# Filling the prologue of a fused attention and feed-forward kernel: eight gate matmuls and one block's transposes moved beside the last scores, another block transposed by DMA, loads two blocks ahead

## The chip, the cores and the metric

The kernel runs on one core of one Trainium2 chip. The metric is the device time in microseconds (us), the median of several executions. A profiled execution also has a span, from its first to its last instruction, about 2 us less than the time. Engines are named as in the profile: PE is TensorE (matmuls), PEld its weight loads, DVE VectorE, ACT ScalarE, POOL GpSimd, SP SyncE, which issues most of the transfers.

Each execution also has a mean granted clock of PE. Most have 0.998 to 1.000 ("full clock" below). Some have 0.991 to 0.996 and take about 1 to 2 us longer, for the same kernel. All are counted as fast, so ratios include them.

## The reference

Sigmoid attention (8 batches, 12 heads, 448 positions, 64 per head), then a gated feed-forward layer with 768 model columns and 1536 hidden ones:

```python
scores = q @ k.T / sqrt(64) - log(448)
attn   = sigmoid(scores)
x      = (attn @ v)  # heads side by side: 3584 tokens x 768
out    = (relu(x @ w_gate) * (x @ w_val)) @ w_out
```

Inputs and the result are float32; the kernel computes in float16 with float32 accumulation. What matters here: attention is one sigmoid for each score, so ACT is busy with it, while the feed-forward part is almost all PE work.

## The kernel before

The 12 heads of a batch are three blocks of four heads; block n belongs to batch n // 3. The scores of a block come in seven chunks; chunk c of block n is one "step". Before any feed-forward product of batch 0 can be finished, the 21 steps of blocks 0, 1 and 2 must be done: this is the prologue. Then the feed-forward part of batch b runs on PE, with the attention steps of batch b+1 placed between its matmuls.

A block must be loaded, cast to float16 and transposed (k and q) before its first score. Blocks 0 to 6 were transposed on PE, later ones by DMA.

```python
def feed(i):                      # after attention step i
    n, c = divmod(i, NCH)         # NCH = 7 steps to a block
    m = n + LOAD_AHEAD            # LOAD_AHEAD = 3
    if c == 0 and NPRO <= m < NB: # NPRO = 6
        load_all(m)
    m = n + 1
    if c == 0 and NPRO <= m < NB:
        cast_block(m)             # on POOL
    if c == 4 and NPRO < m < NB:
        dma_transposes(m)
    if c == 5 and NBLK < m <= NPRO:
        transposes(m, "k")        # 7 on PE into PSUM, one DVE copy out
        transposes(m, "q")

# ... cut: loads of blocks 0 to 2, casts of block 0
order = halves("g", 0) + halves("u", 0) + [3] + halves("g", 1) + ...   # g, u, o: w_gate, w_val, w_out; a number: a block

for i in range(NP0 + 2):          # the prologue, NP0 = 21
    n, c = divmod(i, NCH)
    if n < NBLK:
        scores(n, c)              # 4 matmuls, then a sigmoid on ACT
    while done <= i - (4 if i < NP0 - 4 else 2):
        values(done // NCH, [done % NCH])
        done += 1
    # ... cut: casts and transposes of blocks 1 and 2
    if 13 <= i < NP0:
        start_next()              # the next load of "order", and its cast

# feed-forward of batch b
for step, cost in enumerate(ffn(b)):
    t += cost
    if b == 0 and step == 12:     # block 3
        transposes(NBLK, "k")
        transposes(NBLK, "q")
    # ... cut: starts loads, and places attention steps by t
```

One PSUM pool of four banks (`wkp`) serves the transposes, the value accumulators (two a block), and the gate, value and output products. A tile of the pool gets a bank only when the last reader of its old tile is done, and PE takes its matmuls in program order: one that waits for a bank (in a run below for 0.33 us) holds up all that stand behind it.

Of the kernel before, what the change touches and what calls it, by code (L numbers as in the profile page):

```python
# [9 lines left out]
FP32 = mybir.dt.float32  # L10
FP16 = mybir.dt.float16
AOP = mybir.AluOpType
AF = mybir.ActivationFunctionType
# [3 lines left out]
def kernel(  # L17
# [10 lines left out]
    nc = tc.nc  # L28

    B, H, S, D = q.shape  # L30
    DM, DF = moe_w_gate.shape
    P = 128
    HB = 4
    NBLK = H // HB
# [58 lines left out]
    def load_all(n: int):  # L93
        load_block(n, ("k", k, 0, NCH, nc.sync), ("q", q, 0, NCH, nc.sync), ("v", v, 0, NCH, nc.sync))
# [45 lines left out]
    def dma_transposes(n: int):  # L140
        for nm in ("k", "q"):
            h16 = qk16.pop((nm, n))
            t2 = qkTp.tile([P, NCH, 2, KC], FP16, tag="qkT", name=f"{nm}T")
            nc.sync.dma_start_transpose(
                t2[:].rearrange("p c h k -> p c (h k)"), h16[:].rearrange("p c r d -> p (c r d)")
            )
            qkT[nm, n] = t2

    def transposes(n: int, nm: str, *engines, cut=(0, NCH)):
        h16 = qk16.pop((nm, n))  # L150
        tr = wkp.tile([P, NCH, 2, KC], FP16, tag="wk", name="tr")
        for c in range(cut[0], cut[-1]):
            nc.tensor.transpose(tr[:, c], h16[:, c, :, :], ident[:])  # L153
        t2 = qkT.get((nm, n)) or qkTp.tile([P, NCH, 2, KC], FP16, tag="qkT", name=f"{nm}T")
        for c0, c1, eng in zip(cut, cut[1:], engines or (nc.vector,)):
            if eng is nc.scalar:
                eng.copy(t2[:, c0:c1], tr[:, c0:c1])
            else:
                eng.tensor_copy(t2[:, c0:c1], tr[:, c0:c1])
        qkT[nm, n] = t2  # L160
# [22 lines left out]
    def values(n: int, chunks):  # L183
        if chunks[0] == 0:
            PT[n] = [wkp.tile([P, 512], FP32, tag="wk", name="pv_ps") for _ in range(2)]
        pv = PT[n]
        t = v16[n]
        for c in chunks:
            pt = PT.pop((n, c))
            for pr, r, o in ((0, 0, 0), (0, 64, 64), (1, 64, 0), (1, 0, 64)):  # L190
                nc.tensor.matmul(  # L191
                    pv[pr][o : o + 64, 0:S],
                    t[r : r + 64, pr, c * D : (c + 1) * D],
                    pt[r : r + 64, pr, :],
                    start=(c == 0),
                    stop=(c == NCH - 1),
                    tile_position=(r, o),
                    skip_group_check=True,
                )
        if chunks[-1] == NCH - 1:  # L200
            b, i = divmod(n, NBLK)
            for pr in range(2):
                x = xTp.tile([P, S], FP16, tag="xT", name="xT")
                nc.vector.tensor_scalar(  # L204
                    out=x[:], in0=pv[pr][:, 0:S], scalar1=XSCALE, scalar2=None, op0=AOP.mult
                )
                xT[b, 2 * i + pr] = x
            PT.pop(n)
            v16.pop(n)
# [1 line left out]

    MM_US = 0.189

    def up(b: int, f: int):
        j, jj = divmod(f, FG)
        ps = []
        for w in (wg[j], wv[j]):
            acc = wkp.tile([P, 512], FP32, tag="wk", name="gv_ps")
            for dc in range(NDC):
                nc.tensor.matmul(  # L220
                    acc[:, 0:S],
                    w[:, dc, jj * P : (jj + 1) * P],
                    xT[b, dc][:],
                    start=(dc == 0),
                    stop=(dc == NDC - 1),
                )
                if dc < NDC - 1:
                    yield MM_US
            ps.append(acc)
            if len(ps) == 1:  # L230
                g_sb = gsbp.tile([P, S], FP32, tag="gsb", name="gate_sb")
                nc.scalar.activation(g_sb[:], acc[:, 0:S], AF.Relu)  # L232
                yield MM_US
        o = (b % NHALF) * S
        nc.vector.tensor_tensor(  # L235
            out=hT[f][:, o : o + S], in0=g_sb[:], in1=ps[1][:, 0:S], op=AOP.mult
        )
        yield MM_US

    def down(col0: int):  # L240
# [37 lines left out]

    def ffn(b: int):
        for f in range(NFC):  # L280
            yield from up(b, f)
        for col0 in blocks128(b):
            yield from down(col0)

# [1 line left out]
        return NFC * 2 * NDC * MM_US + len(blocks128(b)) * NFC * (DM / 2400.0 + 0.004)  # L286


    LOAD_AHEAD = 3
    NPRO = 2 * NBLK  # L290

    def cast_block(n: int):
        cast_qk(n, "q", nc.gpsimd)
        cast_qk(n, "k", nc.gpsimd)
        cast_v(n, nc.gpsimd)

    def feed(i: int):

        n, c = divmod(i, NCH)
        m = n + LOAD_AHEAD  # L300
        if c == 0 and NPRO <= m < NB:
            load_all(m)
        m = n + 1
        if c == 0 and NPRO <= m < NB:
            cast_block(m)
        if c == 4 and NPRO < m < NB:
            dma_transposes(m)
        if c == 5 and NBLK < m <= NPRO:
            transposes(m, "k")
            transposes(m, "q")  # L310

    state = {"pass": NBLK * NCH}
    def visit():
# [26 lines left out]
    with tc.manual_schedule():  # L340
        nc.scalar.activation(warm[:], bias_t[:], AF.Sigmoid)

        sp, act = nc.sync, nc.scalar
        load_block(0, ("q", q, 0, NCH, sp), ("k", k, 0, 4, act), ("k2", k, 4, NCH, sp), ("v", v, 0, NCH, act))
        load_block(1, ("k", k, 0, NCH, sp), ("q", q, 0, NCH, act), ("v", v, 0, NCH, sp))
        load_block(2, ("k", k, 0, NCH, act), ("q", q, 0, NCH, sp), ("v", v, 0, NCH, sp))

        def halves(kind, j):
            return [(kind, j, 0), (kind, j, 1)]

        order = halves("g", 0) + halves("u", 0) + [3] + halves("g", 1) + halves("u", 1)
        order += [4] + halves("g", 2) + halves("u", 2) + halves("o", 0) + [5]
        order += halves("o", 1) + halves("o", 2)

        def start_next():
            what = order.pop(0)
            if isinstance(what, int):
                load_all(what)
                cast_block(what)
            else:  # L360
                load_w(*what)
                cast_w(*what, nc.gpsimd)

        new_fill()
        filler(*[512] * 10)
        cast_qk(0, "q", nc.vector, nc.scalar, cut=(0, 4, NCH))
        cast_qk(0, "k", nc.vector, nc.scalar, cut=(0, 2, 4))
        transposes(0, "q")
        filler(128, 128)
        transposes(0, "k", nc.scalar, nc.vector, cut=(0, 2, 4))  # L370
        new_fill()
        filler(128, 128, 128)
        cast_qk(0, "k2", nc.vector, cut=(4, NCH))
        for n in range(NBLK):
            cast_v(n, nc.gpsimd)
        for _ in range(4):
            start_next()


        NP0 = NBLK * NCH  # L380
        done = 0
        for i in range(NP0 + 2):
            n, c = divmod(i, NCH)
            if n < NBLK:
                scores(n, c)
# [3 lines that stand above are left out]
            if i == 2:  # L389
                qk16["k", 0] = qk16.pop(("k2", 0))  # L390
                transposes(0, "k", nc.vector, cut=(4, NCH))
            if 1 <= i <= 3:
                filler(256)
            if c == 1 and n + 1 < NBLK:
                cast_qk(n + 1, "k", nc.vector)
                cast_qk(n + 1, "q", nc.vector)
            if c in (3, 5) and n + 1 < NBLK:
                transposes(n + 1, "k" if c == 3 else "q")
            if 13 <= i < NP0:
                start_next()  # L400

        for b in range(B):
            total = ffn_us(b)
            todo = []
            if b + 1 < B:
                count = 3 * NBLK + (2 if b == 0 else 0)
                lo = 4.0 if b == 0 else 0.0
                todo = [lo + (k + 0.5) * (total - lo) / count for k in range(count)]
            t = 0.0
            for step, cost in enumerate(ffn(b)):  # L410
                t += cost
                if b == 0 and step == 12:
                    transposes(NBLK, "k")
                    transposes(NBLK, "q")
                if order and step % 8 == 0:
                    start_next()
                if todo and t >= todo[0]:
                    todo.pop(0)
                    visit()
            for _ in todo:  # L420
                visit()
# [29 lines left out]
```

## Time and profile before

| | before |
|---|---|
| time, median of 3 | 434.99 us (434.75 to 435.08) |
| span of the profiled execution | 432.7 us, clock 0.999 |
| PE busy | 421.4 us, 97% |
| prologue: start of the last values | 26.75 us |
| first output matmul | 62.60 us |
| last cast of w_out | 65.96 to 67.43 us |

The prediction shows most lines of the profile. The page's second part, from which it starts, divides the span into 40 slices and gives the busy share of each engine in tenths.

### The profile page before, as it was taken

What the parts mean: (1) busy time and instruction counts of PE and PEld (TensorE: products, weight loads), DVE (VectorE), ACT (ScalarE), POOL (GpSimd) and SP (SyncE); (2) the same over time, 40 slices, a digit from 0 to 9 for tenths busy, and PEclk for the clock granted to TensorE, in tenths of its full rate; (3) what the DMA queues carried; (4) which work ended last, traced back from release to release, by engine and by line L of the source; (5) the groups of instructions that cost most, each with busy time, mean ns of one, the idle gap of its engine ahead of it and who ended that gap; (6) DMA issues with size and microseconds to landing.
All of it is one profiled execution on the core that took longest, in us unless ns stands there. A gap on an engine that the chain in (4) does not pass through costs nothing.

```text
span 432.7 us, 7894 instructions
## 1 busy us (share of the span) xinstructions
PE 421.4 (97%) x3296; PEld 214.6 (50%) x3296; DVE 99.5 (23%) x168; ACT 235.4 (54%) x325; POOL 105.6 (24%) x139
## 2 busy tenths in 40 slices
PE   7789999999999999999999999999999999999996
PEld 3344455544555445544455445554455544455554
DVE  3432332132202222122211233023220232212210
ACT  5955656655556656555546555565555556532221
POOL 2687669222301403113021133013030100000000
PEclk9999999999999999999999999999999999999999
DMA  8999997891238920695217932299114320030014
GB/s 302 385 385 385 388 394 261 229 268 46 42 77 238 300 45 2 172 244 163 42 42 198 251 126 44 53 234 294 22 21 111 79 44 2 17 94 1 2 36 111
DMA packets 62516, 66.52 MB, mean 154 GB/s; under 512 B 33936, under 2 KB 52752, under 8 KB 62480
## 3 DMA queue, kind: packets, MB, share of 16 engines
q1 hardware_dynamic: 61232, 64.17, 50.8%
q10 hardware_dynamic: 1248, 1.84, 1.2%
q8 instruction: 26, 0.43, 0.4%
q14 instruction: 10, 0.08, 0.1%
HBM read 47.19 MB, written 11.01 MB: 134 GB/s over the span
## 4 chain that ended last, share of the span: by engine, by line
PE 86%; DMA 6%; ACT 3%; POOL 2%; issue 1%; DVE 1%; SPq 0%; DVEq 0%; POOLq 0%
PE gv_ps L220 47%; PE y_ps L252 25%; PE qk_ps L167 8%; PE pv_ps L191 6%; DMA st_wo<-in_moe_w_out_dram 5%; ACT PT L177 3%; DMA st_k<-in_k_dram 2%; POOL wo L137 1%; PE tr L153 0%; POOL wg L137 0%; DVE xT L204 0%; SPq L90 0%; DVE h16q L105 0%; POOL v L112 0%; POOL v L114 0%
## 5 line engine op out<-in xcount | busy, mean ns | idle before, releaser
L177 ACT ACTIVATE PT<-qk_ps,bias_t 128x896 f16<-128x896 f32 x168 | 158.1, 1011 | 58.5 <-PE qk_ps L167 58.5
L220 PE MATMUL gv_ps<-xT,wv 128*128 128x448 f16 x576 | 127.8, 353 | 0.0
L220 PE MATMUL gv_ps<-xT,wg 128*128 128x448 f16 x576 | 127.4, 353 | 0.2 <-DVE xT L204 0.2
L252 PE MATMUL y_ps<-wo,hT 128*128 128x512 f16 (+2 forms) x684 | 114.5, 323 | 0.4 <-POOL wo L137 0.4
L232 ACT ACTIVATE gate_sb<-gv_ps 128x448 f32<-128x448 f32 x96 | 52.3, 544 | 91.6 <-PE gv_ps L220 91.6
L235 DVE TENSOR_TENSOR hT<-gate_sb,gv_ps 128x448 f16<-128x448 f32 x96 | 59.6, 621 | 168.1 <-PE gv_ps L220 137.5
L252 PEld LDWEIGHTS <-hT 128*128 128x128 f16 x684 | 64.2, 98 | 48.6 <-issue 8.2
L220 PEld LDWEIGHTS <-wv 128*128 128x128 f16 x576 | 54.6, 98 | 57.3 <-issue 8.6
L220 PEld LDWEIGHTS <-wg 128*128 128x128 f16 x576 | 54.9, 98 | 53.5 <-issue 5.7
L112 POOL CAST v<-st_v 128x448 f16<-128x448 f32 x24 | 13.5, 562 | 180.4 <-PE pv_ps L191 171.1
L204 DVE TENSOR_SCALAR xT<-pv_ps 128x448 f16<-128x448 f32 x48 | 27.7, 619 | 127.1 <-PE pv_ps L191 127.1
L167 PE MATMUL qk_ps<-qT,kT 64*64 64x448 f16 x672 | 51.4, 360 | 4.7 <-ACT PT L177 3.9
L264 ACT ACTIVATE ysb<-y_ps 128x512 f32<-128x512 f32 (+2 forms) x56 | 27.4, 489 | 39.8 <-PE y_ps L252 39.5
L191 PE MATMUL pv_ps<-PT,v 64*64 64x448 f16 x672 | 39.0, 349 | 0.8 <-ACT PT L177 0.8
L167 PEld LDWEIGHTS <-kT 64*64 64x64 f16 x672 | 15.4, 105 | 34.7 <-issue 30.1
L105 POOL CAST h16q<-st_q 128x896 f16<-128x896 f32 x21 | 19.6, 932 | 40.2 <-DMA kT<-h16k 32.8
L191 PEld LDWEIGHTS <-v 64*64 64x64 f16 x672 | 20.0, 107 | 12.6 <-issue 1.8
L105 POOL CAST h16k<-st_k 128x896 f16<-128x896 f32 x21 | 19.6, 932 | 0.4 <-DMA qT<-h16q 0.3
L114 POOL CAST v<-st_v 64x448 f16<-64x448 f32 x24 | 13.7, 570 | 1.0
L113 POOL CAST v<-st_v 64x448 f16<-64x448 f32 x24 | 13.4, 560 | 1.5
L137 POOL CAST wv<-st_wu 128x1536 f16<-128x1536 f32 x6 | 8.8, 1470 | 3.4 <-DMA st_wu<-in_moe_w_val_dram 3.4
L137 POOL CAST wg<-st_wg 128x1536 f16<-128x1536 f32 x6 | 8.8, 1467 | 2.0 <-DMA st_wg<-in_moe_w_gate_dram 1.7
(25 smaller groups left out, 47.9 us busy)
## 6 DMA issues: line engine op xcount, KB each, us to landing
out_dram<-ysb SPq DMA_DIRECT2D x54, 192.0 KB, 2.7
st_q<-in_q_dram SPq DMA_DIRECT2D x23, 448.0 KB, 5.9
st_v<-in_v_dram SPq DMA_DIRECT2D x23, 448.0 KB, 6.6
st_k<-in_k_dram SPq DMA_DIRECT2D x22, 448.0 KB, 5.0
st_wg<-in_moe_w_gate_dram SPq DMA_DIRECT2D x6, 768.0 KB, 12.2
st_wu<-in_moe_w_val_dram SPq DMA_DIRECT2D x6, 768.0 KB, 12.2
st_wo<-in_moe_w_out_dram SPq DMA_DIRECT2D x6, 768.0 KB, 11.4
st_v<-in_v_dram ACTq DMA_DIRECT2D x1, 448.0 KB, 5.4
```

Source lines behind the costliest of these rows:

```text
L105: eng.tensor_copy(o, i)
L114: eng.tensor_copy(t[64:128, 1], st[0:64, 1])
L137: eng.tensor_copy(dst, st[:])
L167: nc.tensor.matmul(ps[o : o + 64, bank, 0:S], kT[r : r + 64, c, h, :], qT[r : r + 64, :, h, :], start=True, stop=True, tile_position=(r, o ...
L177: nc.scalar.activation(pt[:], ps[:, :, 0:S], AF.Sigmoid, bias=bias_t[:], scale=qk_scale)
L191: nc.tensor.matmul(pv[pr][o : o + 64, 0:S], t[r : r + 64, pr, c * D : (c + 1) * D], pt[r : r + 64, pr, :], start=(c == 0), stop=(c == NCH ...
L204: nc.vector.tensor_scalar(out=x[:], in0=pv[pr][:, 0:S], scalar1=XSCALE, scalar2=None, op0=AOP.mult)
L220: nc.tensor.matmul(acc[:, 0:S], w[:, dc, jj * P : (jj + 1) * P], xT[b, dc][:], start=(dc == 0), stop=(dc == NDC - 1),)
L232: nc.scalar.activation(g_sb[:], acc[:, 0:S], AF.Relu)
L235: nc.vector.tensor_tensor(out=hT[f][:, o : o + S], in0=g_sb[:], in1=ps[1][:, 0:S], op=AOP.mult)
L252: nc.tensor.matmul(y[:, 0:w], hT[f][:, o : o + P], wo[f // FG][:, f % FG, c0 : c0 + w], start=(f == 0), stop=(f == NFC - 1),)
L264: nc.scalar.activation(dst, y[:, 0:w], AF.Copy, scale=OUT_SCALE)
```

## The change

Its intent: the prologue is paced by ACT and leaves PE with holes. Put PE work there that would otherwise stand in the PE-bound part: the transposes of block 3 (its load moved forward to be there in time) and the first four of six matmuls of two gate products. Take the transposes of block 6 off PE altogether. And load blocks later, so that w_out gets through sooner.

```diff
@@ values: the last tile of block 2 is scaled on ACT instead of DVE
+                if pr and n == NBLK - 1:
+                    nc.scalar.activation(x[:], pv[pr][:, 0:S], AF.Copy, scale=XSCALE)
@@ up: a product can be begun elsewhere; f=0 also has 4 value matmuls ahead
+    def gv_part(b, f, w, dcs): ...   # cut: a bank at the first call, then the matmuls dcs
+            if b == 0 and f < 2:
+                yield from up(b, f, 4, 4 if f == 0 else 0)
@@ feed
-        m = n + LOAD_AHEAD
-        if c == 0 and NPRO <= m < NB:
-            load_all(m)
-        if c == 4 and NPRO < m < NB:
+        if c == 4 and NPRO <= m < NB:
             dma_transposes(m)
+        if c == 4 and NPRO <= m + 1 < NB:
+            load_all(m + 1)
-        if c == 5 and NBLK < m <= NPRO:
+        if c == 5 and NBLK < m < NPRO:
@@ order of the loads
-        order = halves("g", 0) + halves("u", 0) + [3] + halves("g", 1) + halves("u", 1)
+        order = halves("g", 0) + [3] + halves("u", 0) + halves("g", 1) + halves("u", 1)
@@ prologue
+            if i == 14:
+                cast_qk(NBLK, "k", nc.vector)
+            if i == 15:
+                transposes(NBLK, "k")
+                cast_qk(NBLK, "q", nc.vector)
+            if i == 16:
+                transposes(NBLK, "q")
+            if i in (17, 18):
+                gv_part(0, i - 17, wg, [0, 1])
+            if i in (20, 21):
+                gv_part(0, i - 20, wg, [2, 3])
@@ feed-forward of batch 0
-                if b == 0 and step == 12:
-                    transposes(NBLK, "k")
-                    transposes(NBLK, "q")
```

Cut: block 3 no longer cast by POOL except for v; two weight halves fewer started before the prologue, and the other loads from step 11 on instead of 13.

More of the change, by code (lines that the diff above doesn't have):

```diff
@@ L203, in values @@
                 x = xTp.tile([P, S], FP16, tag="xT", name="xT")
-                nc.vector.tensor_scalar(
-                    out=x[:], in0=pv[pr][:, 0:S], scalar1=XSCALE, scalar2=None, op0=AOP.mult
-                )
+                if pr and n == NBLK - 1:
+                    nc.scalar.activation(x[:], pv[pr][:, 0:S], AF.Copy, scale=XSCALE)
+                else:
+                    nc.vector.tensor_scalar(
+                        out=x[:], in0=pv[pr][:, 0:S], scalar1=XSCALE, scalar2=None, op0=AOP.mult
+                    )
                 xT[b, 2 * i + pr] = x
@@ L212, with gv_part, up @@
     MM_US = 0.189
-    def up(b: int, f: int):
-        j, jj = divmod(f, FG)
-        ps = []
-        for w in (wg[j], wv[j]):
-            acc = wkp.tile([P, 512], FP32, tag="wk", name="gv_ps")
-            for dc in range(NDC):
-                nc.tensor.matmul(
-                    acc[:, 0:S],
-                    w[:, dc, jj * P : (jj + 1) * P],
-                    xT[b, dc][:],
-                    start=(dc == 0),
-                    stop=(dc == NDC - 1),
-                )
-                if dc < NDC - 1:
-                    yield MM_US
-            ps.append(acc)
-            if len(ps) == 1:
-                g_sb = gsbp.tile([P, S], FP32, tag="gsb", name="gate_sb")
-                nc.scalar.activation(g_sb[:], acc[:, 0:S], AF.Relu)
+    begun: dict = {}
+    def gv_part(b: int, f: int, w, dcs):
+        key = (b, f, w is wg)
+        if key not in begun:
+            begun[key] = wkp.tile([P, 512], FP32, tag="wk", name="gv_ps")
+        j, jj = divmod(f, FG)
+        for dc in dcs:
+            nc.tensor.matmul(
+                begun[key][:, 0:S],
+                w[j][:, dc, jj * P : (jj + 1) * P],
+                xT[b, dc][:],
+                start=(dc == 0),
+                stop=(dc == NDC - 1),
+            )
+        return begun[key]
+    def up(b: int, f: int, gate_done=0, val_first=0):
+        if val_first:
+            gv_part(b, f, wv, range(val_first))
+        for dc in range(gate_done, NDC):
+            gate = gv_part(b, f, wg, [dc])
+            if dc < NDC - 1:
+                yield MM_US
+        g_sb = gsbp.tile([P, S], FP32, tag="gsb", name="gate_sb")
+        nc.scalar.activation(g_sb[:], gate[:, 0:S], AF.Relu)
+        yield MM_US
+        for dc in range(val_first, NDC):
+            val = gv_part(b, f, wv, [dc])
+            if dc < NDC - 1:
                 yield MM_US
         o = (b % NHALF) * S
-        nc.vector.tensor_tensor(
-            out=hT[f][:, o : o + S], in0=g_sb[:], in1=ps[1][:, 0:S], op=AOP.mult
-        )
+        nc.vector.tensor_tensor(out=hT[f][:, o : o + S], in0=g_sb[:], in1=val[:, 0:S], op=AOP.mult)
         yield MM_US
@@ L280, in ffn @@
         for f in range(NFC):
-            yield from up(b, f)
+            if b == 0 and f < 2:
+                yield from up(b, f, 4, 4 if f == 0 else 0)
+            else:
+                yield from up(b, f)
         for col0 in blocks128(b):
@@ L286, in ffn_us @@
         return NFC * 2 * NDC * MM_US + len(blocks128(b)) * NFC * (DM / 2400.0 + 0.004)
-    LOAD_AHEAD = 3
     NPRO = 2 * NBLK
@@ L305, in feed @@
             cast_block(m)
-        if c == 4 and NPRO < m < NB:
-            dma_transposes(m)
-        if c == 5 and NBLK < m <= NPRO:
+        if c == 5 and NBLK < m < NPRO:
             transposes(m, "k")
             transposes(m, "q")
+        if c == 4 and NPRO <= m < NB:
+            dma_transposes(m)
+        if c == 4 and NPRO <= m + 1 < NB:
+            load_all(m + 1)
     state = {"pass": NBLK * NCH}
@@ L358, in start_next @@
                 load_all(what)
-                cast_block(what)
+                if what > NBLK:
+                    cast_block(what)
+                else:
+                    cast_v(what, nc.gpsimd)
             else:
@@ L375 @@
             cast_v(n, nc.gpsimd)
-        for _ in range(4):
+        for _ in range(2):
             start_next()
@@ L398 @@
                 transposes(n + 1, "k" if c == 3 else "q")
-            if 13 <= i < NP0:
+            if i == 14:
[9 more added lines that the diff above has]
+                gv_part(0, i - 20, wg, [2, 3])
+            if 11 <= i < NP0:
                 start_next()
```

## The prediction

> **What bounds the kernel now.** I read the busy shares first, then the slices, then the chain that ended last in order of time, then stretches of the timeline. The span of the profiled execution is 432.7 us; the time is 434.99 us.
>
> ```profile
> PE 421.4 (97%) x3296; PEld 214.6 (50%) x3296; DVE 99.5 (23%) x168; ACT 235.4 (54%) x325; POOL 105.6 (24%) x139
> PE   7789999999999999999999999999999999999996
> DMA  8999997891238920695217932299114320030014
> ```
>
> PE (TensorE) is the bound: 97% busy, and its row is below 9 only in the first three slices (the first 32 us) and in the last. The granted clock is full throughout. So whatever takes work off PE after about 27 us shortens the kernel by that work; DVE, ACT and POOL have room. The DMA row says that the transfers are saturated in the first six slices, 65 us at 380 to 394 GB/s. The chain in order of time shows where PE is not the bound:
>
> ```profile
> 23.79 0.71 ACT PT L177
> 24.68 0.72 ACT PT L177
> 25.57 1.14 ACT PT L177
> 26.75 0.43 PE pv_ps L191 x4
> 27.19 1.15 DVE xT L204 x2
> 28.38 1.67 PE gv_ps L220 x8
> 30.05 0.78 PE tr L153 x14
> ...
> 52.16 11.77 DMA st_wo<-in_moe_w_out_dram
> 63.98 1.47 POOL wo L137
> 65.45 0.49 issue
> 65.96 1.48 POOL wo L137
> 67.48 1.79 PE y_ps L252 x13
> ```
>
> Up to 26.75 us ACT sets the pace: one sigmoid (L177) each 0.89 us, 21 of them, and PE has a hole in each step. Then PE runs alone, except that the last half of the last w_out group is loaded and cast (by POOL) only just in time at 67.48. The waits of PE in this stretch are small:
>
> ```profile
> 24.06 0.38 PE L167 MATMUL qk_ps<-qT,kT 64*64 64x448 f16 x4 [0.32 <-ACT PT L177]
> 28.38 0.35 PE L220 MATMUL gv_ps<-xT,wg 128*128 128x448 f16 x1 [0.18 <-DVE xT L204]
> 67.48 0.70 PE L252 MATMUL y_ps<-wo,hT 128*128 128x512 f16 x3 [0.44 <-POOL wo L137]
> ```
>
> The bracket is the idle time just before and its releaser. The first is the hole that the change wants to fill.
>
> **What the Trainium skill says.** "Perfetto Trace Analysis", section Optimization Strategy: where the most contended engine changes over time, interleaving the regimes may help. That is this change; the trace agrees that an ACT-paced regime (to 26.75 us) meets a PE-paced one. The same section says that consistent bubbles on the engine that should be saturated can mean too little SBUF or PSUM for the next tile; no such bubbles are in the PE stretch of before, but I find below that the new prologue runs into just that. "TensorE: Matmul & The Clock Gate", Part 4: a transpose on TensorE goes to PSUM and so needs a DVE copy after; the trace has it, 0.62 us per 128x896 copy (L159). "DMA: Bandwidth & Descriptors", Issuing engines are not separate DMA queues: all issuers share the same 16 DMA engines, so an earlier load only makes another later. The trace agrees: weight halves (768 KB) are cast 2.03 us apart at 385 GB/s.
>
> **The change part by part.**
>
> 1. Block 3 is transposed in the prologue. 14 transposes, 0.78 us of PE at 30.05, leave the PE-bound stretch: **-0.78**.
>
> 2. Eight gate matmuls (two each for f=0 and 1, twice) go into the ACT-paced steps. PE issues one each 0.189 us (six in 1.13 to 1.14): **-1.51**.
>
> 3. Block 6 is transposed by DMA. The chain has 0.89 us for its 14 transposes at 73.63, the timeline 0.80 between starts: **-0.8**. Its DMA transposes (4.2 and 3.1 us to landing at the median) follow in the queue the first output, which I place at 69.3 to 70.4 us; they land near 75 to 76, and the scores that need them come near 78. Hidden, by about 2 us.
>
> 4. Loads two blocks ahead. Before, block 6 (three of 448 KB, 1.19 us each = 3.6 us of a full DMA) was queued ahead of block 5 and the last four w_out halves. Now it comes after them. The last half lands at 65.95 - 3.6 = 62.4, and its cast ends at 63.9 instead of 67.43. The wait at 67.48 can go. From the first output matmul (62.60) to the tenth is 10 x 0.213 us, plus 2.12 us for the scores and values between (62.60 + 0.64 to 65.36), so the wait is 62.60 + 2.13 + 2.12 = 66.85 to 67.48: **-0.63** if w_out is then early enough.
>
> 5. The last tile of block 2 is scaled on ACT and four value matmuls stand ahead of the gates' rest. This should hide the 0.18 us. But four PSUM banks serve this pool. In the built program the value tile takes the bank of block 2's first half, the two begun gates hold two others: it can't start before DVE has read that half.
>
> 6. The price, in the prologue. Steps 14 to 17 now hang on a serial DVE chain, which I follow from measured durations. In before, g0's second half is cast at 19.52, straight on landing. Block 3 now comes next: k lands at about 19.5 + 1.2 = 20.7, q at 21.9 (v 23.1, then w_val 25.1 and 27.1, cast by 28.6). DVE: cast k 20.65 to 21.27 (0.62); PE transposes 21.3 to 21.7, drained 21.9; DVE copies kT to 22.5, casts q 22.5 to 23.1; PE transposes q 23.1 to 23.5. Only then comes the score of step 17, which was at 22.26 and had 0.22 us of slack (sigmoids of this stretch start 0.64 us after the score is issued, it needs 0.44): sigmoid 17 goes from 22.90 to 23.97, **+1.07**. Then the qT copy (23.75 to 24.37) and the tile of block 1 (first half 24.29 to 24.91) run on DVE. The first begun gate takes the bank of that half (the assignment in the built program), so it waits till 24.96, stands ahead of the score of step 18 and puts that at 25.34; sigmoid 18 starts at 25.78 instead of 23.97 + 0.90: **+0.9**. The last two sigmoids follow without loss. The prologue ends 2.0 us later: last values at 28.75 instead of 26.75, block 2's tile on DVE till 29.79, first value matmul at 29.84.
>
> Check against a common point, f=0 and f=1's gates and f=0's values done: before 31.61; after 29.84 + 10 x 0.189 = 31.73. So parts 1, 2, 5 and 6 together give +0.1: the prologue gives back all that it was filled with. From there the PE work is the same up to the w_out wait: output matmuls start at 62.7, the tenth ends at 64.9, a microsecond after the cast at 63.9; the wait is gone.
>
> 7. Later. The shorter f=0 and 1 do not advance the count that places the attention steps, so those of batch 0 come 12 matmuls later, and the last falls at the end of batch 0. Values of block 5 then stand right ahead of batch 1, whose sixth gate matmul needs the second tile at 1.41 us after the values and is reached at 1.25: **+0.16**. From batch 1 on the PE order repeats what it was.
>
> Sum: +0.12 - 0.63 - 0.8 + 0.16 = -1.15 us, to 433.8.
>
> **The rivals.**
>
> (a) The prologue is not stretched: block 3 lands earlier or the chain is shorter than I add up. Then 1.51 + 0.78 count in full up to w_val's second half (cast by 28.6) and w_out: output matmuls reach the wait before 63.9 and are held there, so the gain up to that point is at most 65.46 - 63.9 = 1.56 (65.46 is 67.48 without the 2.02 us of attention work that now comes later). With part 3 and 7: 2.2 us, 432.8. For it: the steps look placed by someone who had a trace. Against: even with q landed in time the chain cast, transpose, copy, cast, transpose costs about 1.5 us.
>
> (b) Block 3 lands later, since w_gate's second half took 2.95 us to come after the first. Each microsecond goes straight into the sigmoids: 1 us later gives 434.8.
>
> (c) PE waits for block 6's DMA transposes: block 6 lands near 65.9, is cast by 66.6, but the transposes stand in the queue behind an output. If they take 2 us more than their median, PE waits a little; a loss of 1 to 2 us gives 435. The longest seen for kT is 5.3.
>
> (d) The later loads starve attention in batches 1 to 7. A block is asked for 2 attention steps, about 9 us, ahead of its cast and lands in 4 to 6 us (median of the stretch after 82 us): hidden.
>
> **Range and chances.** The sum says 433.8, rival (a) 432.8 and (b), (c) 434.8. I lean a little to (a), as the placement looks tuned: 433.5, range 432.3 to 434.9. No step is worth the 8.7 us of 2%.
>
> **What would show it.** Chain: the prologue's last sigmoid starting near 27.5 instead of 25.57, with the DVE copies and casts of block 3 in the chain near 21 to 25. PE waits for DVE at steps 16 to 18. No PE wait for POOL wo; its last cast ending near 63.9. 14 fewer transposes on PE, and no wait of PE for a DMA at block 6. If sigmoids stay 0.89 us apart throughout, part 6 is wrong; if PE waits for kT or qT of block 6, part 3 is.

## More of the kernel before

One line of ACT is needed later, for the sigmoids of the prologue; its columns are explained after the result:

```profile
11.32 15.38 ACT L177 ACTIVATE PT<-qk_ps,bias_t 128x896 f16<-128x896 f32 x17 [0.35 <-PE qk_ps L167]
```

## The result, and the profile after

The changed kernel takes 433.9 us (median of 4, 433.41 to 434.1, all at full clock), the kernel before on the same chip 434.88 us. The ratio is 0.9975, 95% interval 0.9958 to 0.9993. A ratio here is the mean time of one kernel's fast runs over that of the other's of the same rounds, so it is not quite the ratio of the medians. So the change gains about 1 us.

The page of the changed kernel has PE with 14 instructions fewer and 0.6 us less busy:

```profile
PE 420.8 (98%) x3282; PEld 212.8 (49%) x3282; DVE 98.9 (23%) x167; ACT 236.1 (55%) x326; POOL 102.8 (24%) x137
```

Next, ACT in the prologue of the changed kernel, in order of time. The columns are the start, the duration of the merged group, engine, line, operation, output and input, count, and in brackets the idle time before and its releaser:

```profile
11.05 10.88 ACT L177 ACTIVATE PT<-qk_ps,bias_t 128x896 f16<-128x896 f32 x12 [0.68 <-PE qk_ps L167]
22.34 1.01 ACT L177 ACTIVATE PT<-qk_ps,bias_t 128x896 f16<-128x896 f32 x1 [0.41 <-PE qk_ps L167]
24.16 1.01 ACT L177 ACTIVATE PT<-qk_ps,bias_t 128x896 f16<-128x896 f32 x1 [0.81 <-PE qk_ps L167]
25.95 2.89 ACT L177 ACTIVATE PT<-qk_ps,bias_t 128x896 f16<-128x896 f32 x3 [0.78 <-PE qk_ps L167]
```

Before, the last 17 sigmoids stood in one line without a break, 0.9 us apart to the end. Now sigmoids 16, 17 and 18 each wait for PE (0.41, 0.81 and 0.78 us). The reader sees why on DVE, in the same stretch:

```profile
20.55 0.74 DVE L105 CAST h16k<-st_k 128x896 f16<-128x896 f32 x1 [1.32 <-DMA st_k<-in_k_dram]
21.95 0.62 DVE L159 COPY kT<-tr 128x896 f16<-128x896 f16 x1 [0.66 <-PE tr L153]
22.50 0.62 DVE L105 CAST h16q<-st_q 128x896 f16<-128x896 f32 x1
23.77 0.62 DVE L159 COPY qT<-tr 128x896 f16<-128x896 f16 x1 [0.66 <-PE tr L153]
24.31 1.15 DVE L207 TENSOR_SCALAR xT<-pv_ps 128x448 f16<-128x448 f32 x2
```

That is one serial chain: k of block 3 lands and is cast (20.55), PE transposes it, DVE copies kT (21.95), casts q (22.50), PE transposes q, DVE copies qT (23.77), and only then comes the tile of block 1 (24.31), whose bank the first gate needs. On PE, by the same columns:

```profile
21.35 0.57 PE L153 MATMUL tr<-ident,h16k 128*128 128x128 f16 x7 [0.59 <-DVE h16k L105]
...
23.17 0.56 PE L153 MATMUL tr<-ident,h16q 128*128 128x128 f16 x7 [0.75 <-DVE h16q L105]
23.66 0.38 PE L167 MATMUL qk_ps<-qT,kT 64*64 64x448 f16 x4
...
24.98 0.54 PE L226 MATMUL gv_ps<-xT,wg 128*128 128x448 f16 x2
25.45 0.38 PE L167 MATMUL qk_ps<-qT,kT 64*64 64x448 f16 x4
...
28.89 0.38 PE L191 MATMUL pv_ps<-PT,v 64*64 64x448 f16 x4
29.98 0.92 PE L226 MATMUL gv_ps<-xT,wv 128*128 128x448 f16 x4 [0.71 <-DVE xT L207]
```

The transposes wait 0.59 and 0.75 us for casts, the score of step 17 stands behind them (23.66), the first gate starts only at 24.98, and the score of step 18 stands behind that (25.45). The last values start at 28.89 instead of 26.75, and the value product at 29.98 after 0.71 us of waiting for the tile of block 2. Further on, the wait for w_out is gone: in a later stretch the first twelve output matmuls and three more run without a break, and the last cast of w_out starts 3.7 us sooner than before (62.27 instead of 65.96):

```profile
62.85 3.08 PE L265 MATMUL y_ps<-wo,hT 128*128 128x512 f16 x15
...
77.98 0.57 PE L167 MATMUL qk_ps<-qT,kT 64*64 64x448 f16 x8
```

```profile
62.27 1.47 POOL L137 CAST wo<-st_wo 128x1536 f16<-128x1536 f32 x1 [0.55 <-DMA st_wo<-in_moe_w_out_dram]
```

The line at 77.98 holds the first scores of block 6: no bracket, so PE did not wait for its DMA transposes, which the queue had issued at 70.85 and 72.30.

### The profile page after: what moved, and what is told of

The parts are those of the page before. It is cut to its first block, busy times and chain, and to the rows that moved or that the text cites. A ratio compares the mean times of both kernels' runs of the same rounds, so it can differ in the third digit from the quotient of the medians.

```text
span 431.6 us, 7867 instructions
## 1 busy us (share of the span) xinstructions
PE 420.8 (98%) x3282; PEld 212.8 (49%) x3282; DVE 98.9 (23%) x167; ACT 236.1 (55%) x326; POOL 102.8 (24%) x137
## 4 chain that ended last, share of the span: by engine, by line
PE 94%; DMA 4%; DVE 1%; issue 0%; SPq 0%; DVEq 0%
PE gv_ps L226 52%; PE y_ps L265 26%; PE qk_ps L167 9%; PE pv_ps L191 7%; DMA st_k<-in_k_dram 4%; PE tr L153 1%; SPq L90 0%; DVE h16k L105 0%; DVE h16q L105 0%; DVE xT L207 0%; DVE ysb L279 0%; DVE kT L159 0%; DVEq L279 0%
## 5 line engine op out<-in xcount | busy, mean ns | idle before, releaser
L105 POOL CAST h16q<-st_q 128x896 f16<-128x896 f32 x20 | 18.6, 930 | 224.7 <-DMA st_q<-in_q_dram 200.9
L105 POOL CAST h16k<-st_k 128x896 f16<-128x896 f32 x20 | 18.6, 928 | 0.0
```

The lines of the kernel that those rows point to most:

```text
L105: eng.tensor_copy(o, i)
```

## The experiments

The theory: filling the holes costs about as much as it brings, because each piece hangs on DVE and on a bank; the net gain comes from the w_out wait and block 6. The rivals: the filling is where the gain is, or the loads don't matter. Three calls of four kernels each, all correct, with five rounds; each call is on one chip and has its own runs of before.

| label | median | ratio to before (95%) | at full clock: number, median |
|---|---|---|---|
| before, first call | 435.37 | | 5 of 11, 434.68 |
| e1_no_gates | 433.63 | 0.9962 (0.9945 to 0.9978) | 5 of 6, 433.62 |
| e2_no_tr3 | 432.59 | 0.9935 (0.992 to 0.9951) | 6 of 6, 432.59 |
| e3_no_fill | 433.25 | 0.9959 (0.9933 to 0.9984) | 3 of 6, 432.39 |
| e4_block6_early | 436.92 | 1.0034 (1.0014 to 1.0055) | 2 of 6, 435.98 and 436.15 |
| before, second call | 435.01 | | 7 of 11, 434.95 |
| e5_loads_only | 435.24 | 1.0003 (0.9979 to 1.0027) | 3 of 6, 433.81, 434.03, 435.21 |
| e6_dma6_only | 434.06 | 0.9985 (0.997 to 1.0) | 5 of 6, 433.84 |
| e7_spread | 432.44 | 0.9939 (0.9923 to 0.9955) | 4 of 6, 432.23 |
| e8_gates_later | 434.0 | 0.9976 (0.9963 to 0.999) | 3 of 6, 433.34 |
| before, third call | 434.77 | | 8 of 11, 434.73 |
| r_after | 433.76 | 0.9983 (0.9971 to 0.9995) | 4 of 5, 433.70 |
| r_no_tr3 | 432.61 | 0.9949 (0.9937 to 0.996) | 5 of 5, 432.61 |
| r_no_fill | 432.98 | 0.9963 (0.995 to 0.9977) | 5 of 6, 432.98 |
| r_spread | 431.64 | 0.993 (0.9917 to 0.9942) | 5 of 5, 431.64 |

### The gates taken out of the prologue

```diff
-            if i in (17, 18):
-                gv_part(0, i - 17, wg, [0, 1])
-            if i in (20, 21):
-                gv_part(0, i - 20, wg, [2, 3])
-            if b == 0 and f < 2:
-                yield from up(b, f, 4, 4 if f == 0 else 0)
```

> The changed kernel without the eight gate matmuls in the prologue (f=0 and f=1 are as any other). Theory (the filling pays for itself): the begun gates hold up the score of step 18, since the first of them waits for the bank of block 1's tile, so without them the prologue ends about 0.9 us sooner (last values at about 28.0 instead of 28.9), and the gates then fill what is now a 0.7 us wait for the tile of block 2; the eight matmuls return to the PE-bound stretch for 1.5 us. Net 433.9, within 0.3 of the changed kernel. Rival (the gates were free, as holes were filled): 1.5 us slower than the changed kernel, 435.4.

Measured: 433.63, not 435.4. Eight matmuls worth 1.5 us of PE moved back into the PE-bound part cost nothing (the four value matmuls ahead of f=0's gate went with them). ACT in the prologue of this version shows the delay that went with them:

```profile
23.98 1.01 ACT L177 ACTIVATE PT<-qk_ps,bias_t 128x896 f16<-128x896 f32 x1 [0.81 <-PE qk_ps L167]
25.14 2.80 ACT L177 ACTIVATE PT<-qk_ps,bias_t 128x896 f16<-128x896 f32 x3 [0.15 <-PE qk_ps L167]
```

Sigmoid 18 comes 1.16 us after sigmoid 17, not 1.79 as in the changed kernel (24.16 to 25.95). The last values start at 27.99, as expected. The rival falls: the gates were not free.

### The transposes of block 3 put back

```diff
             if i == 15:
-                transposes(NBLK, "k")
                 cast_qk(NBLK, "q", nc.vector)
-            if i == 16:
-                transposes(NBLK, "q")
@@ feed-forward of batch 0
+                if b == 0 and step == 12:
+                    transposes(NBLK, "k")
+                    transposes(NBLK, "q")
```

> The changed kernel with the transposes of block 3 put back to where they were before, beside the first gates; the gates in the prologue stay. Theory: the score of step 17 no longer waits for the chain of cast, transpose, copy on DVE, so the prologue ends about 1.8 us sooner (last values near 27.1 instead of 28.9), the 14 transposes cost 0.8 us of PE again: net 1.0 us faster than the changed kernel, 432.9, with no wait of PE for the casts of block 3. Rival (moving PE work into the prologue is a gain): 0.8 us slower, 434.7.

Measured 432.59 at first and, beside the changed kernel on one chip in the third call (the same kernel under a new label), 432.61 against 433.76:

> The changed kernel again, on one chip with the three versions that were measured on two chips, as some executions there had a lower mean granted clock (0.992 to 0.996) and 1 to 2 us more. Executions with a full clock: 433.9, ratio to before 0.9975 as in the first measurement.

> The version with block 3 transposed beside the gates, on the same chip as the changed kernel. Theory (the chain on DVE costs more than it moves): 1.0 to 1.4 us faster than the changed kernel at full clock, 432.5 to 432.9. Rival (the earlier difference was one of chips): the same as the changed kernel.

So undoing this part gains 1.1 us, as the theory said to within 0.1, though it puts 0.8 us back on PE. In the third call's trace the sigmoids are on time up to number 17, and the one interruption left is the begun gate's, 0.50 us on ACT:

```profile
13.77 10.00 ACT L177 ACTIVATE PT<-qk_ps,bias_t 128x896 f16<-128x896 f32 x11
24.27 2.89 ACT L177 ACTIVATE PT<-qk_ps,bias_t 128x896 f16<-128x896 f32 x3 [0.50 <-PE qk_ps L167]
```

That gate waits 0.33 us for DVE's read of block 1's tile, and it and its second matmul stand ahead of the next score, which starts at 23.77:

```profile
23.30 0.54 PE L226 MATMUL gv_ps<-xT,wg 128*128 128x448 f16 x2 [0.33 <-DVE xT L207]
```

### No filling at all

Both edits above together.

> The changed kernel with nothing filled into the prologue: no gates, no transposes of block 3 there. The order of the loads, block 6 by DMA and the later loads stay. Theory: sigmoids are 0.89 us apart to the end (last values near 26.5 to 26.8), and what is left of the change is the wait for w_out (0.6) and the 14 transposes of block 6 (0.8): 433.4 to 433.5, so 0.4 faster than the changed kernel. Rival (the filling is where the gain is): close to the kernel before or 1 us slower than the changed one, 434.9.

> The version without any filling, on the same chip. At full clock 432.4 as before (theory by the sum: 0.5 faster than the changed kernel; measured on the other chip 1.5 faster). If the sparse prologue invites the drop of the granted clock, again about half of its runs show a lower clock, and few of the changed kernel and of the version without block 3's transposes; if the chip decides, all kernels of this call show it alike.

Measured: 433.25 with three of six executions at lower clock, the other three at 432.3 to 432.4; in the third call 432.98, 0.7 us faster than the changed kernel at full clock (433.70). The direction is the theory's in both calls: without its filling, the change gains more. The sigmoids run to the end without a break. The size (0.5 expected) came out at 1.5 and 0.7. Part of it is a term that I had too small: before, the gate's sixth matmul waited for block 2's second tile, 0.18 us by the bracket, but by the starts of the matmuls 0.34 us (27.07 to 28.56 for six, against 1.15 us in this version, where ACT takes that tile).

The traces account for the rest. In the third call's run PE reaches the first output matmul at 62.61, as before (62.60), and after the same attention work twenty output matmuls follow without a wait:

```profile
65.37 3.32 PE L265 MATMUL y_ps<-wo,hT 128*128 128x512 f16 x20
```

From the first output matmul to the first gate of batch 1 PE takes 18.54 us before (62.60 to 81.14) and 17.17 here (62.61 to 79.78). These 1.37 us and the 0.34 make 1.7, and the third call measured 1.75 against before at full clock (432.98 against 434.73). The first call's run has the same 17.16 us. That it is 0.6 us faster comes from a part that no edit touches: its last values start at 26.52, those of the third call at 27.11, after PE has waited 0.54 and 1.00 us for DVE's copy of block 1's k near 10 us.

The gates alone (this version against the one with only block 3 put back) bring 0.4 us in the third call and cost 0.2 in the first, at full clock: not clear of such scatter.

### The load of block 6 early again

```diff
+        if c == 0 and n == NBLK:
+            load_all(NPRO)
-        if c == 4 and NPRO <= m + 1 < NB:
+        if c == 4 and NPRO < m + 1 < NB:
             load_all(m + 1)
```

> The changed kernel with the load of block 6 queued ahead of block 5 and the last w_out halves again, as before the change. Theory: those halves land 3.6 us later, the last cast ends near 67.4, PE reaches that output matmul at about 65.0 and waits 2.3 us for POOL: 436.2. Rival (loads are hidden, their order is worth nothing): 433.9.

Measured: 435.98 and 436.15 at full clock, 436.25 and three times 437.6 to 437.8 at lower clock. PE waits twice, 0.83 and 1.33 us, in all 2.2 as worked out:

```profile
65.51 0.59 PE L265 MATMUL y_ps<-wo,hT 128*128 128x512 f16 x2 [0.83 <-POOL wo L137]
67.43 1.65 PE L265 MATMUL y_ps<-wo,hT 128*128 128x512 f16 x5 [1.33 <-POOL wo L137]
```

So in the changed kernel the order of the loads is worth about 2.3 us: with the old order it would be slower than the kernel before. This profiled run also shows what the slower executions are. The stretches, with PE's busy time and matmuls in them, the granted clock, the DMA share and GB/s:

```profile
66.00:67.00 1.00, 0.10 (x1) 1.00 0.00 0
67.00:68.00 1.00, 0.57 (x2) 0.58 0.00 0
68.00:69.00 1.00, 1.00 (x5) 0.50 0.00 0
69.00:70.00 1.00, 1.00 (x13) 0.50 0.00 0
70.00:71.00 1.00, 1.00 (x20) 0.71 0.00 0
71.00:72.00 1.00, 1.00 (x22) 1.00 0.00 0
```

From 67.16, in the second wait, the clock is halved for 3.41 us, and PE loses about half of that. One such drop lowers the mean clock by 0.5 x 3.41 / 432 = 0.004; each of the six profiled executions at 0.995 or 0.996 has one. By the same sum 0.991 and 0.992 would be two drops, an estimate that no profiled run shows.

### Two parts alone, on the kernel before

The later loads alone:

```diff
-        m = n + LOAD_AHEAD
-        if c == 0 and NPRO <= m < NB:
-            load_all(m)
+        if c == 4 and NPRO <= m + 1 < NB:
+            load_all(m + 1)
```

> The kernel before with one part of the change alone: loads two blocks ahead, so that block 6 comes after w_out. Theory: the wait of PE for the last w_out cast (0.44 shown, 0.63 worked out) goes and nothing else: 434.3 against 434.9. Rival: no change, 434.9, or slower because block 6 comes late for its transposes.

Inconclusive by time: 435.24 with an interval that holds both, and half of the executions at lower clock. The trace is clear on the wait: twenty output matmuls follow each other from 66.55 without the bracket that stood at 67.48 before. From the first output matmul to the first gate of batch 1 this run takes 17.94 us instead of 18.54, 0.60 of the 0.63 worked out. A clock drop had made PE 1.2 us late for its first output, but the last cast ends at 63.64, so PE would have found it ready at its usual time too.

```profile
66.55 3.32 PE L252 MATMUL y_ps<-wo,hT 128*128 128x512 f16 x20
```

Block 6 by DMA alone:

```diff
-        if c == 4 and NPRO < m < NB:
+        if c == 4 and NPRO <= m < NB:
             dma_transposes(m)
-        if c == 5 and NBLK < m <= NPRO:
+        if c == 5 and NBLK < m < NPRO:
```

> The kernel before with one part of the change alone: block 6 transposed by DMA. Theory: 14 transposes less on PE, hidden transfers: 434.1, 0.8 faster than before. Rival: PE waits for the transposed block or the later output pays for it: 434.9.

Measured 434.06, ratio 0.9985: 0.7 us by the ratio, 1.1 us at full clock (433.84 against 434.95), where 0.8 was expected. No wait of PE for the transposed block shows in the trace.

### The gates two steps later

```diff
-            if i in (17, 18):
-                gv_part(0, i - 17, wg, [0, 1])
-            if i in (20, 21):
-                gv_part(0, i - 20, wg, [2, 3])
+            if i in (19, 20):
+                gv_part(0, i - 19, wg, [0, 1])
+            if i in (21, 22):
+                gv_part(0, i - 21, wg, [2, 3])
```

> The changed kernel with its first gate matmuls at steps 19 and 20 instead of 17 and 18, and the second ones at 21 and 22; all else the same. Theory: by step 19 the bank of block 1's tile is free, so the score of step 18 is not held up (sigmoid 18 starts 0.9 us after sigmoid 17, not 1.8), while the delay at step 17 stays: last values near 28.0, 0.9 us faster than the changed kernel, 433.0. Rival (the bank does not matter; the delay is of PE time or DVE casts): 433.9.

By time this missed: 434.0 over all, the three executions at full clock 433.24, 433.34 and 433.95, the ratio that of the changed kernel. In the trace (this execution had a clock drop earlier, so only intervals compare) sigmoid 18 comes 1.16 us after 17 (25.70 and 26.86), as in the run without gates; 0.9 was expected. That the bank held the score up, as the theory had it, is not shown: this run and the one without gates take away both the gate's wait for the bank and the gate's own time. The changed kernel's trace tells them apart. There the last value matmul ahead of the gate starts at 24.67 and takes PE 0.19 us, so of the time till the gate's start (24.98, which is 0.05 us after DVE has read the tile) some 0.12 us are the bank's. The gate's two matmuls then hold the score up for 0.47 us (24.98 to 25.45). The 0.27 us that are left in both runs fit another bank: the matmuls for the second tile of block 2's values start 0.05 us after the copy of qT has ended, at 24.45 in the changed kernel, at 24.27 without gates and at 25.99 here.

The 0.6 us so freed can't be told from the scatter of this call.

### The filling, spread so that no sigmoid waits

```diff
-            if i == 14:
+            if i == 15:
                 cast_qk(NBLK, "k", nc.vector)
-            if i == 15:
-                transposes(NBLK, "k")
-                cast_qk(NBLK, "q", nc.vector)
-            if i == 16:
-                transposes(NBLK, "q")
-            ...                       # cut: the gates of the changed kernel
+            if i == 16:
+                transposes(NBLK, "k")
+            if i == 18:
+                cast_qk(NBLK, "q", nc.vector)
+            if i == 19:
+                gv_part(0, 0, wg, [0, 1])
+            if i == 20:
+                transposes(NBLK, "q")
+            if i == 21:
+                gv_part(0, 0, wg, [2, 3])
+            if i == 22:
+                gv_part(0, 1, wg, [0, 1, 2, 3])
@@ ffn
-                yield from up(b, f, 4, 4 if f == 0 else 0)
+                yield from up(b, f, 4)
```

Here DVE reads block 1's tile before it casts q; each transpose and each gate comes a step or more after what it needs; only one gate holds a bank; and f=1's gate fills the wait for block 2's tile.

> The changed kernel with the filling spread so that no step waits: cast of block 3's k at step 15, its transposes at step 16, cast of q at step 18, its transposes at step 20; only the gate of f=0 is begun at steps 19 and 21, four matmuls of f=1's gate come after the last values, where the tile of block 2 is awaited; no value matmuls ahead. Theory (the price came from the order on DVE and from the banks, not from filling as such): sigmoids 0.89 us apart to the end, last values near 26.5, no wait of PE for DVE after them, common point (gates of f=0 and 1 and values of f=0 done) at 29.4 instead of 31.9; 2.4 us faster than the changed kernel, 431.5. Rival (PE work in the prologue delays the sigmoids wherever it stands): no better than the version without filling, 433.5.

> The version with the filling spread, on the same chip. Theory: at full clock 2.0 to 2.4 us faster than the changed kernel, 431.5 to 431.9, and the fastest of the four. Rival (filling gives nothing however it is placed): equal to the version without filling.

Measured 432.44 on the chip of the second call (two of six at lower clock), and 431.64 in the third call, with all five at full clock, beside 433.76 for the changed kernel: 2.1 us faster, ratio to before 0.993. It is also 1.3 us faster than the version without filling (432.98), so filling does bring something where nothing waits for it. It beats every other version of its call. In the third call's trace all sigmoids stand in one line without a break, though PE does the same transposes between them:

```profile
13.04 13.71 ACT L177 ACTIVATE PT<-qk_ps,bias_t 128x896 f16<-128x896 f32 x15
```

```profile
21.80 0.56 PE L153 MATMUL tr<-ident,h16k 128*128 128x128 f16 x7
...
25.51 0.56 PE L153 MATMUL tr<-ident,h16q 128*128 128x128 f16 x7
...
26.80 0.38 PE L191 MATMUL pv_ps<-PT,v 64*64 64x448 f16 x4
27.12 1.32 PE L226 MATMUL gv_ps<-xT,wg 128*128 128x448 f16 x6
...
29.79 1.30 PE L226 MATMUL gv_ps<-xT,wv 128*128 128x448 f16 x6
```

No bracket after the last values at 26.80; f=1's values begin at 29.79 instead of 31.87, which is the common point of the prediction (29.4 was expected). So the rival, that PE work in the prologue delays sigmoids wherever it stands, falls too.

### What the clock did

I expected that the kernel without filling would lose clock more often. In the three calls 13 of 33 executions of before had a mean clock under 0.998, 4 of 12 without filling, 1 of 9 of the changed kernel (with the four of its first measurement), none of 11 with block 3 put back, 2 of 11 with the filling spread. The third call alone had 1 of 6 without filling and 1 of 5 of the changed kernel. That does not tell a cause from chance.

The traces tell more. Apart from the end of the span, where PE runs out of work, six of the 14 profiled runs have one drop each. It always lasts 3.41 us, and it always begins a whole number of 3.41 us after the start of the trace's clock record (4.0 to 6.3 us into the span, different in each execution). In the 3.41 us up to each drop PE was busy for 45 to 60% of the time, as the profile counts it. Of the 293 other such stretches up to 80 us in the 14 traces only one was as low without a drop (57%, in the run without gates). So the traces fit this: the share of time that PE works in a stretch decides, and where the stretches fall is chance, which makes the same kernel lose clock in one execution and not in the next. No experiment tested it. In the third call's run of the changed kernel the drop began at 11.00 us, after PE had waited 1.02 us for block 1's cast and in a wait of 0.52 us for its copy, thus before any edit.

## Why the prediction was right

The range, the sign and the working sum (433.8) agree with the measured 433.9; only the lean from 433.8 to 433.5 was not needed. Point by point:

- **Part 6, the price of the prologue**, was the risky step and it was right in kind and nearly in size. Predicted: last values at 28.75, common point 31.73. Measured: 28.89 and 31.87. Delay of sigmoid 17 over its turn: 1.07 predicted, 0.93 measured (24.16 - 22.34 - 0.89); of 18: 0.9 predicted, 0.90 measured. One term was left out: sigmoid 16 also came 0.5 us late (1.4 us after its predecessor, the last of twelve, which ended at 21.93 and took 1.01), as k was cast at 20.55 to 21.29 while the steps of this execution stood 0.28 us earlier than before. In all 2.4 us instead of 2.0, of which 2.14 show in the last values, as the steps stood earlier. The prediction's own times held a part of this: k's transposes end at 21.7, 0.34 us after the turn of step 16's score, which had 0.22 us of slack. The experiments show the two causes apart: without the transposes the delay at step 17 goes, with the gates gone or two steps later the one at step 18 shrinks. Within the latter, the gates' own time (0.47 us) weighs more than the wait for the bank (0.12).
- **Parts 1 and 2** (0.78 and 1.51 us) are real PE work, but given back by part 6, as the sum said: taking the gates out left the time as it was, and putting the transposes back gained 1.1 us.
- **Part 5** was rightly distrusted: the value matmuls ahead waited 0.71 us for the bank. The old wait was mis-sized, 0.34 us instead of 0.18.
- **Part 4**, the w_out wait: the last cast was predicted to end at 63.9 and ends at 63.7; PE does not wait. The run with the old load order costs about 2.3 us, as worked out. That the later loads alone are worth 0.63 us on the kernel before is not shown by time; the trace of that run shows 0.60.
- **Part 3**: no wait for block 6. Its DMA transposes land at 75.89 and 76.72, its scores start at 77.98, predicted "75 to 76" and "near 78": hidden by 1.3 us instead of 2. The time of the part alone holds 0.8 within its scatter.
- **Part 7**: the first gate of batch 1 takes 1.47 us for its six matmuls where others take 1.30, 0.17 us for the predicted 0.16.
- **The sum** is right by its parts, not by errors that cancel. The first output matmul starts at 62.85, 0.25 us later than before (0.12 predicted). From there to the first gate of batch 1 PE takes 17.15 us instead of 18.54 (1.39 less; 1.43 predicted), and that gate 0.17 more: 0.97 us in all, and 0.98 measured.
- **One reading** was loose: "the first six slices" at 380 to 394 GB/s include the first, which has 302. Nothing rests on it.
- **The rivals**: (a) did not happen in this kernel. It described what a better placement would do; the spread version is that, and goes beyond its limit of 432.8, because rival (a) let PE wait for w_out: in the spread version ten output matmuls are issued by 63.0, attention work fills PE until 65.0, and the last cast ends at 63.8 meanwhile. My ground for leaning to it, that the steps look placed from a trace, was no evidence. (b), (c) and (d) did not happen: k was cast at 20.55 (20.65 predicted), and PE has no wait for a DMA in the whole trace.

## What to carry to other kernels

A hole on an engine is free only for work whose operands and buffers are ready at that point and which is done before the next piece of the pacing chain is due; in a program-ordered queue a piece that waits takes everything behind it along. Before moving work into holes, write down the chain on the other engine that feeds it, and which buffer each tile takes over from whom; then place each piece a step after both are free. And where one change has a part that costs and a part that gains, time the parts apart: here the version that keeps the gains and spreads the filling gains three times as much as the whole (3.1 against 1.0 us in the third call, at full clock).

## What the Trainium skill lacked or had wrong

- "TensorE: Matmul & The Clock Gate", Part 1, HAM oscillation: it sums the rule up as no idle gaps of PE above about 3.4 us (the section after it tells of short idles that do the same, without a figure). Here the clock fell to 0.50 for 3.41 us in six profiled runs, and no wait of PE just before was longer than 1.6 us: in the 3.41 us up to the drop PE was busy for 45 to 60%. The drop after waits of 0.83 and 1.33 us (the run with block 6 loaded early) cost 1.7 us: three of the four executions at lower clock took 437.6 to 437.8 us, the two at full clock 436.0 and 436.2.
- "TensorE: Matmul & The Clock Gate", Part 4: it gives about 275 ns for a 128x128 transpose within a kernel, the length of one. Here one has 219 ns in the profile (its end is modelled), but 14 in a row take 0.80 us between starts, 57 ns each. For work in a row that spacing is what PE pays, and this part gives none.
